# Spatial products moved into the second half of their own batch, thresholds placed by position: threshold attention followed by a gated layer on one core

## The chip, the cores and the metric

One core of a Trainium2 chip (trn2). The metric is the device time of one execution in microseconds. "Span" is the time between first and last instruction of a profiled execution; it is some 2 us shorter than the device time.

In the lines of the profile PE is TensorE (matrix products and transposes), ACT is ScalarE, DVE is VectorE, POOL is GpSimd and SP is the queue that issues DMA. PSUM is the memory into which PE writes its results. The *granted clock* is the share of TensorE's full clock that the profile shows as granted.

## The reference, cut to what matters

Shapes: 8 batches, 8 heads, 576 positions, head size 64; the gated layer maps 512 to 1024 and back to 512.

```python
scores = scale * q @ k^T                                  # per head, 576 x 576
thresh = max(scores, -1) - tau                            # keep what lies within tau of the maximum
attn = softmax(where(scores >= thresh, scores, -1e9))
x = (attn @ v)                                            # heads side by side: 576 x 512 per batch
h = relu(x @ w_in); u, v = h[:, :512], h[:, 512:]
v_n = (v - mean(v)) / sqrt(var(v) + 1e-6)
v_s = w_spatial @ v_n + b_spatial                         # 576 x 576 over positions
out = (u * v_s) @ w_out
```

## The kernel before: the parts that matter

Attention runs in 144 steps: 32 pairs of heads, each with blocks c = 0 to 3 of 128 query rows, and one step c = 4 for the remaining 64 rows of every two pairs. Four pairs make a batch, hence 18 steps per batch. I call the place of a step within its batch its *position*, 0 to 17: pair 0 has 0 to 3, pair 1 has 4 (c = 4) and 5 to 8, pair 2 has 9 to 12, pair 3 has 13 (c = 4) and 14 to 17.

Into these steps the gated layer of an earlier batch is woven as small jobs on PE: v (five jobs: values and their normalization), u (five), s (five spatial products) and o (four output products). Each job takes a bank of PSUM from a pool of **two**, and the bank is free again when an engine has copied the result out:

```python
ps_f = ctx.enter_context(tc.tile_pool(name="ps_f", bufs=2, space=PSUM))   # two banks for all jobs
ps_s = inner.enter_context(tc.tile_pool(name="ps_s", bufs=2, space=PSUM)) # two score tiles of three banks

ORDER = "vsvsvsvssuvuouououo"      # one job per step from step LAG = 26 on, 19 in 18 steps
for b in range(B):
    for j, t in enumerate(ORDER):
        g = LAG + PER * b + j      # step; position (j + 8) % 18
        job = (f, b - (t in "so"), n[t])    # s and o belong to the batch before
```

A step issues its scores, then its jobs; copies by ScalarE ("act") and VectorE ("dve") stand at fixed places:

```python
def step(i, c, fs):
    s = scores(i, c)
    for kind, mm, ev in fs[:2]:            # the first two jobs, one bank each
        mm()
        if kind == "act": ev()             # ScalarE copies, behind what it has queued already
    nc.vector.tensor_reduce(out=nm, in_=s, op=ALU.max, negate=True)
    # ... VectorE copies of the first two jobs; delayed squares of v ...
    if on_act(i, c):                       # threshold on ScalarE: Prelu twice, one Exp of 1152
        # ...
    else:                                  # Exp twice; VectorE masks in the next step
        # ...
    if unmasked: mask()                    # VectorE, for the step before
    for kind, mm, ev in fs[2:]:            # a third job needs the first job's bank
        mm()
        # ...

def on_act(i, c):
    return c in (2, 4) or c == 0 and 0 < i < 6
```

After step 143 the *tail* runs what is left of batches 6 and 7, with eight banks, as many as the two job banks and the two score tiles of three banks make in the steps.

## Time and profile before

Median 481.5 us of 4 runs (480.25 to 484.56). I cut the run at the starts of the row maximum on VectorE, of which each step has exactly one:

| stretch | us | what it holds |
|---|---|---|
| start to step 26 | 78.2 | attention of batch 0 and half of 1 |
| steps 26 to 43 | 52.6 | first batch of the gated layer, without s and o before the change |
| steps 44 to 133, per 18 steps | 55.4 | five full batches |
| step 134 to the last maximum | 28.5 | a half period |
| last maximum to the end | 41.3 | the tail |

A period holds 47 to 50 us of ScalarE's and VectorE's work and 52.8 of PE's. The lines are in the prediction.

### The profile page before, as it was taken

How to read it: one execution, taken by the hardware profiler on the slowest of the kernel's cores; microseconds unless marked ns; L12 is line 12 of the kernel's file. 1: busy time of each engine (PE TensorE's matmuls, PEld its weight loads, DVE VectorE, ACT ScalarE, POOL GpSimd, SP SyncE). 2: the span in 40 equal slices, each digit the busy share in tenths (PEclk: the TensorE clock that was granted, in tenths of full speed). 3: DMA queues.
4: the chain of work that ended last, by engine and by line, in shares of the span. 5: the costliest groups of instructions: out<-in, count | busy, mean ns of one | idle time of the engine just before them, and what ended most of it. 6: DMA issues, size and time to landing. Idle time of an engine off the chain costs nothing.

```text
span 477.7 us, 9895 instructions
## 1 busy us (share of the span) xinstructions
PE 447.0 (94%) x3646; PEld 239.6 (50%) x3691; DVE 410.2 (86%) x563; ACT 389.9 (82%) x677; POOL 225.9 (47%) x403
## 2 busy tenths in 40 slices
PE   7788888889999999999999999999999999999995
PEld 5344444445545555454555545545554545545542
DVE  4989888989889988999889989899889998898573
ACT  4899899989879897888979798788978888897251
POOL 3553344895448543574417642565336744252021
PEclk9999999999999999999999999999999999999999
DMA  7989999979888899988978998998997989777522
GB/s 242 238 182 184 217 221 219 196 148 210 172 182 194 196 210 219 196 172 173 215 192 199 181 206 191 204 171 180 200 225 171 186 183 212 149 113 111 150 95 104
DMA packets 227568, 88.49 MB, mean 185 GB/s; under 512 B 197056, under 2 KB 221760, under 8 KB 227520
## 3 DMA queue, kind: packets, MB, share of 16 engines
q1 hardware_dynamic: 226864, 86.98, 85.4%
q8 instruction: 29, 0.48, 0.4%
q0 software_dynamic: 160, 0.52, 0.3%
q10 hardware_dynamic: 496, 0.36, 0.2%
q14 instruction: 19, 0.16, 0.1%
HBM read 33.31 MB, written 9.44 MB: 89 GB/s over the span
## 4 chain that ended last, share of the span: by engine, by line
PE 49%; ACT 22%; DVE 20%; issue 6%; DMA 2%; POOL 0%; POOLq 0%; DVEq 0%; ACTq 0%
PE s L566 14%; DVE negm L604 10%; DVE p L585 7%; ACT e L621 6%; ACT e L627 5%; PE f L294 4%; PE f L245 4%; PE s L561 4%; PE f L535 4%; PE f L476 3%; ACT sq L458 2%; ACT vrel L444 2%; ACT p L623 2%; PE f L506 2%; PE f L289 2%
## 5 line engine op out<-in xcount | busy, mean ns | idle before, releaser
L604 DVE TENSOR_REDUCE negm<-s 128x2 f32<-128x1152 f32 x144 | 194.8, 1353 | 32.2 <-PE s L566 31.8
L566 PE MATMUL s<-qkT 64*128 64x512 f32 (+1 forms) x640 | 161.9, 636 | 0.0
L585 DVE SCALAR_TENSOR_TENSOR p<-e,ctau 128x1152 bf16<-128x1152 f32 x91 | 133.5, 1468 | 1.2 <-ACT e L627 1.2
L627 ACT ACTIVATE e<-s,negm 128x576 f32<-128x576 f32 x182 | 124.9, 741 | 6.2 <-DVE negm L604 6.0
L621 ACT ACTIVATE e<-s,negm 128x576 f32<-128x576 f32 x106 | 73.0, 743 | 14.4 <-DVE negm L608 9.3
L561 PE MATMUL s<-kd,qkT 128*128 128x128 f32 (+1 forms) x320 | 64.5, 304 | 12.1 <-ACT e L627 6.6
L268 POOL COPY kd<-qkT 64x64 f32<-64x64 f32 x62 | 28.2, 455 | 99.5 <-ACT qkT L263 97.7
L561 PEld LDWEIGHTS s<-kd,qkT 128*128 128x128 f32 (+1 forms) x320 | 44.2, 179 | 30.9 <-ACT e L627 15.7
L566 PEld LDWEIGHTS s<-qkT 64*128 64x128 f32 (+1 forms) x640 | 41.9, 174 | 18.2 <-issue 2.7
L452 POOL TENSOR_SCALAR nmean<-sm 128x1 f32<-128x1 f32 (+1 forms) x35 | 15.7, 449 | 68.4 <-ACT vrel L444 61.5
L294 PEld LDWEIGHTS <-pT 128*128 128x128 bf16 x1024 | 41.8, 97 | 8.0 <-issue 5.6
L294 PE MATMUL f<-v,pT 128*128 128x65 bf16 x992 | 44.9, 194 | 0.0
L623 ACT ACTIVATE p<-e 128x1152 bf16<-128x1152 f32 x37 | 43.0, 1163 | 1.2
L136 POOL COPY qn<-ql 128x640 f32<-128x640 f32 x31 | 33.5, 1081 | 16.4 <-DMA ql<-in_k_dram 11.5
L464 POOL TENSOR_SCALAR vn<-vrel,rs,nm 128x512 bf16<-128x512 f32 (+1 forms) x34 | 29.9, 880 | 3.7
L289 PE MATMUL f<-v,pT 128*128 128x130 bf16 x124 | 27.2, 219 | 4.4 <-ACT qkT L252 2.3
L506 PE MATMUL f<-wsT,vn 128*128 128x512 bf16 x119 | 30.7, 379 | 0.3
L252 ACT COPY qkT<-f 128x512 f32<-128x512 f32 x31 | 18.3, 589 | 14.8 <-PE f L245 14.8
L476 PE MATMUL f<-xT,w_in 128*128 128x512 bf16 x97 | 27.8, 381 | 1.6 <-DVE xn L303 0.8
L303 DVE TENSOR_TENSOR xn<-f,r 128x256 bf16<-128x256 f32 x62 | 26.3, 425 | 2.1
L434 PE MATMUL f<-w_in,xT 128*128 128x512 bf16 x102 | 27.5, 380 | 0.3
L444 ACT ACTIVATE vrel<-f 128x512 f32<-128x512 f32 (+1 forms) x34 | 20.1, 592 | 7.4 <-PE f L260 3.0
(168 smaller groups left out, 642.9 us busy)
## 6 DMA issues: line engine op xcount, KB each, us to landing
vl<-in_v_dram SPq DMA_DIRECT2D x16, 512.0 KB, 4.5
ql<-in_q_dram SPq DMA_DIRECT2D x15, 512.0 KB, 4.5
kl<-in_k_dram SPq DMA_DIRECT2D x15, 512.0 KB, 4.5
out_dram<-o SPq DMA_DIRECT2D x20, 256.0 KB, 3.2
uT<-in_moe_w_in_dram SPq DMA_DIRECT2D x3, 512.0 KB, 6.2
uT<-in_moe_w_spatial_dram SPq DMA_DIRECT2D x2, 576.0 KB, 5.1
vl<-in_v_dram SPq DMA_DIRECT2D x16, 64.0 KB, 4.3
pT<-p SPq DMA_TRANSPOSE x64, 5.5
```

What stands on the lines that cost most here:

```text
L136: nc.gpsimd.tensor_copy(out=t, in_=ld_ring[i // 2 % 2][w][:, 2 * (i % 2):2 * (i % 2) + 2].rearrange("p h c d -> p c h d"))
L289: nc.tensor.matmul(out=t[:, at:at + 130], lhsT=pt[:, 4, :], rhs=vt[:, 4:6, :].rearrange("p b d -> p (b d)"), start=True, stop=False)
L294: nc.tensor.matmul(out=t[:, at + 65 * h:at + 65 * h + 65], lhsT=pt[:, 5 * h + j, :], rhs=vt[:, 6 * h + j, :], start=False, stop=(h == 1 an ...
L476: nc.tensor.matmul(out=t, lhsT=w_in[:, m, f * P:(f + 1) * P], rhs=xts[b][:, m, 0:512], start=(m == 0), stop=(m == 3))
L506: nc.tensor.matmul(out=t, lhsT=vn[:, c, f * P:(f + 1) * P], rhs=wsT[:, c, 0:512], start=(c == 0), stop=(c == 4))
L561: nc.tensor.matmul(out=view(s[rows], 512, [[448, 2], [1, 64]]), lhsT=qks[n][:, 0, m], rhs=kd_ring[n % 2], start=True, stop=True)
L566: nc.tensor.matmul(out=s[rows, 1024 * h:1024 * h + 512], lhsT=qks[n][hs, 0, m], rhs=qks[n][hs, 1, 0:512], start=True, stop=True)
L585: nc.vector.scalar_tensor_tensor(out=pt[:, c % 2, :], in0=ef, scalar=ctau, in1=ef, op0=ALU.is_ge, op1=ALU.mult)
L604: nc.vector.tensor_reduce(out=nm, in_=s, axis=AX.X, op=ALU.max, negate=True)
L621: nc.scalar.activation(out=e[:, h, :], in_=s[:, h, :], func=ACT.Prelu, bias=nm[:, h:h + 1], scale=by, alpha=1e30)
L623: nc.scalar.activation(out=pr_ring[i // 2 % 2] if c == 4 else p_ring[2 * (i % 2) + c // 2][:, c % 2], in_=e.rearrange("p h s -> p (h s)"), ...
L627: nc.scalar.activation(out=e[:, h, :], in_=s[:, h, :], func=ACT.Exp, bias=nm[:, h:h + 1])
```

## The change

The intent: let the spatial products of a batch follow in the second half of its own 18 steps, beside the u jobs, and put its output products beside the next batch's v jobs, so that the tail has less left; and put ScalarE's thresholds (which relieve VectorE) into the half where the spatial products load VectorE. The spatial weights must then be ready earlier.

```diff
-        return c in (2, 4) or c == 0 and 0 < i < 6
+        return c == 4 or (c in (0, 2) and i % 4 < 2 if i > 6 else c == 2 or c == 0 and 0 < i < 6)
 ...
-                   ((20, 25, 30), load_ws), ((24, 26, 29, 31, 34), shape_ws),
-                   ((36, 41, 46, 51), load_w_o), ((39, 44, 49, 54), shape_w_o)):
+                   ((19, 22, 28), load_ws), ((23, 25, 27, 30, 33), shape_ws),
+                   ((32, 34, 37, 40), load_w_o), ((35, 38, 41, 44), shape_w_o)):
 ...
-    ORDER = "vsvsvsvssuvuouououo"
+    ORDER = "vovovovovuuusususss"
 ...
-            if t in "uv" or b:
+            if t != "o" or b:
-                job = (f, b - (t in "so"), n[t])
+                job = (f, b - (t == "o"), n[t])
 ...
-        jobs.setdefault((29, 33, 34, 42, 44)[j], []).append((ws_pe, j))
+        jobs.setdefault((29, 31, 33, 35, 36)[j], []).append((ws_pe, j))
 ...   (and the tail's list: batch 6's s jobs come out of ORDER, o and the last v are gone)
```

Per period the thresholds at positions 11 and 16 go to VectorE and those at 0 and 5 go to ScalarE.

More of the change, by code (lines that the diff above doesn't have):

```diff
@@ L860 @@
         run(last[0], pv_rest(NPAIR // 2 - 1), *last[1:3], x_pe(NPAIR - 2), *last[3:6],
-            pv(NPAIR - 1, 0), *last[6:], pv(NPAIR - 1, 1), moe_s(Z - 1, 0), moe_s(Z - 1, 1),
-            x_pe(NPAIR - 1, True), *[moe_s(Z - 1, j) for j in range(2, 5)])
+            pv(NPAIR - 1, 0), last[6], pv(NPAIR - 1, 1), last[7], x_pe(NPAIR - 1, True), last[8])
+        assert len(last) == 9
         rest = last_gmlp(Z)
```

## The prediction

> **What bounds the kernel now.** I read the page first: the engines' shares, then the chain that ended last.
>
> ```profile
> PE 447.0 (94%) x3646; PEld 239.6 (50%) x3691; DVE 410.2 (86%) x563; ACT 389.9 (82%) x677; POOL 225.9 (47%) x403
> ...
> PE 49%; ACT 22%; DVE 20%; issue 6%; DMA 2%; POOL 0%; POOLq 0%; DVEq 0%; ACTq 0%
> ```
>
> Three engines are nearly full and the chain passes among them. The next question is whether 94% on PE is real. The list of the chain in order of time shows the loop: the same piece of PE work comes back once per batch.
>
> ```profile
> 245.98 1.09 PE f L506 x5
> ...
> 301.19 1.08 PE f L506 x5
> ...
> 356.83 1.09 PE f L506 x5
> ...
> 412.04 1.09 PE f L506 x5
> ```
>
> The distances are 55.2, 55.6 and 55.2 us: one batch of attention, 18 steps, with one batch of the gated layer woven in. The table by stretches cuts the run there (cuts are at starts of the row maximum on DVE, one per step):
>
> ```profile
> 78.23:130.85 52.62, 48.18 (x418) 26.77 (x423) 47.30 (x59) 47.77 (x88) 33.76 (x57) 1.00 0.89 185
> ...
> 241.85:297.06 55.21, 54.16 (x442) 28.83 (x448) 49.38 (x64) 47.43 (x85) 27.59 (x49) 1.00 0.91 194
> ...
> 437.80:477.70 39.90, 34.38 (x275) 17.61 (x276) 22.06 (x53) 15.36 (x29) 5.57 (x7) 1.00 0.42 119
> ```
>
> The columns are length, then busy time of PE, weight load, DVE, ACT, POOL. The first row is the only batch period without spatial and output products (there is no batch before the first); the last row is the tail after the last step, where the rest of the gated layer runs alone.
>
> Because PE's ends are modelled, I priced PE by distances between starts in its timeline, two in the loop and six in the tail:
>
> ```profile
> 271.31 0.46 PE L561 MATMUL s<-kd,qkT 128*128 128x128 f32 x2
> ...
> 272.76 0.66 PE L245 MATMUL f<-identf,qn 128*128 128x128 f32 x4
> ```
> ```profile
> 440.34 1.03 PE L476 MATMUL t<-xT,w_in 128*128 128x512 bf16 x4
> 441.21 1.03 PE L535 MATMUL t<-w_o,gT 128*128 128x512 bf16 x4
> 442.07 1.03 PE L476 MATMUL t<-xT,w_in 128*128 128x512 bf16 x4
> ...
> 449.88 1.24 PE L506 MATMUL f<-wsT,vn 128*128 128x512 bf16 x5
> 450.96 0.75 PE L511 MATMUL f<-wsT,vn 128*128 128x64 bf16 x20
> 451.76 3.40 PE L661 MATMUL t<-w_in,xT 128*128 128x512 bf16 x15
> ```
>
> The scores of a step take 1.45, a u, v or o job 0.86, an s job 1.08 (its last, of 64 columns, 0.59; the last u 0.47), a weighing with the values 0.60, the transposes for one pair 1.04. Per period: 18 x 1.45 + 10 x 0.60 + 4 x 1.04 + v 4.3 + u 3.9 + s 4.9 + o 3.4 = 52.8. So **PE is occupied for about 52.8 of 55.2 to 55.6 us**, and idles only 2.3 to 2.8 per period. In the tail it hardly idles until its last product.
>
> **What the Trainium skill says.** "Perfetto Trace Analysis", section "Identifying the Most-Contended Engine", warns that matmul busy time is no measure of headroom; hence the pricing by starts. Here it agrees with the busy column within 1.4 us per period. "TensorE: Matmul & The Clock Gate", section "Back-to-back issue gap", gives N/2.4 + 2.5 ns for an isolated matmul (216 ns at 512 columns), and 131 ns sustained. The trace has 0.86/4 = 215 ns in a stream, so the first figure holds here and the second doesn't: no hidden speed is left in PE. "ScalarE: Activation LUTs", section "What ACT_TABLE_LOAD costs", gives 186 + 0.833 N ns with immediate operands: 1146 ns for the thresholding Exp of 1152 elements, against 1163 in the trace. "Perfetto Trace Analysis", section "Matmuls", asks that groups rotate through banks so that evacuation overlaps; only two such banks serve these jobs here, and most of PE's small waits are for one (0.44 and 0.37 us per period before the third job of two steps).
>
> **The change, part by part.**
>
> ```profile
> L604 DVE TENSOR_REDUCE negm<-s 128x2 f32<-128x1152 f32 x144 | 194.8, 1353 | 32.2 <-PE s L566 31.8
> ...
> L585 DVE SCALAR_TENSOR_TENSOR p<-e,ctau 128x1152 bf16<-128x1152 f32 x91 | 133.5, 1468 | 1.2 <-ACT e L627 1.2
> ...
> L623 ACT ACTIVATE p<-e 128x1152 bf16<-128x1152 f32 x37 | 43.0, 1163 | 1.2
> ```
>
> *Thresholds by position.* A step thresholded on ACT costs ACT 1.16 more and DVE about 1.42 - 0.2 less. Counting the condition over the 32 pairs: before, 32 (c=2) + 5 (c=0) + 16 (c=4) = 53 steps; after, for i up to 6, 7 + 5, for later pairs 12 x 2, and 16: 52. The totals don't move (7 of 18 steps per period in both); only the place does: they now lie in the half of the batch that holds u and s.
>
> *Order.* The 19 jobs of a period stay the same: PE's 52.8 us remain. What moves is DVE's load: before, two neighbouring steps (the eighth and ninth of the order) hold maximum, mask, weighing and spatial gating, 1.35 + 1.42 + 0.75 + 0.69 = 4.2 and 1.35 + 1.42 + 0.2 + 0.6 + 0.42 = 4.0 us of DVE, 8.2 against 6.4 of PE. In the trace they take 4.1 and 3.7 us between row maxima, against a mean of 3.08. Afterwards the heaviest such pair is 2.8 + 4.3 = 7.1 of DVE against 6.9 of PE. A sum of the largest load over every two neighbouring steps falls by 0.6 us per period; over three or more steps it is even. I take **-0.5 per period**, over 5.5 periods: **-2.8**.
>
> *First batch.* Its five spatial products (4.9 us of PE) move from after it into its own period. That one had 48.5 of work in 52.6; it gets 53.4 and should take 55.5 or so: **+3.0**. The weights' loads, a few steps earlier, are small beside that.
>
> *Tail.* Of batch 6, the tail keeps u1 to u4 and its five s jobs, and loses the last v job and four o jobs: 5 x 0.86 = 4.3 of PE; the half period before it gets 0.6 lighter (it holds v and o, not v and s). That is the same 4.9 us that went to the first batch. Not all comes back, though. The view of the mean's readers shows this:
>
> ```profile
> L452 POOL TENSOR_SCALAR nmean<-sm x35: 182/192/1415, 79.3 to 439.8; 128x1 f32<-128x1 f32 x28, 64x1 f32<-64x1 f32 x7
> L458 ACT ACTIVATE sq<-vrel,nmean x34: 708/711/734, 84.5 to 431.1; 128x512 bf16<-128x512 f32 x28, 64x512 bf16<-64x512 f32 x6
> ```
>
> Seven last-rows means, but six squares: the delayed normalization of batch 6's last v job is queued after the queue was emptied, so the kernel before never executes it and uses stale rows (too small an effect on the output to notice, by the 0.01/576 weights). Now that job is in the last but one step, and its normalization does run, behind the last step's Exp (done at about 439.2): square 0.9, then POOL's small operations 1.0 and the 0.8 us write, so about 442.3. The first s job can come as early as 436.3 + 0.86 + 0.60 + 0.86 = 438.6 and its fifth product must wait: **2.8 us of PE idle**, in place of the work that left. The last transposed weights land at 445.7 in the trace, which then binds no more. Net for the end: -4.3 - 0.6 + 2.8 + 0.5 for the shorter cover of the last transposes = **-1.6**.
>
> Sum: 482.5 - 2.8 + 3.0 - 1.6 = 481.1. I shade this to 480.5, as my tail wait could be partly covered.
>
> **Rivals.** (a) *The balance pays fully*: if DVE's heavy steps cause most of PE's 2.3 to 2.8 us of idling per period, 5.5 periods give up to -14, or 468. Against it: those waits are spread over a dozen places of 0.05 to 0.44 us, mostly bank evictions by ACT, which the change doesn't remove. (b) *A new collision*: v with its square and o are all ACT's, so in the first half ACT's evictions come later; or the step with v, weighing and s wants a third bank. Another 0.5 us per period would give 486. For it: two banks only; against: before has as many three-job steps. (c) *The tail gives all 4.9 us and the first batch hides its own*: 475 or so; against: the first batch's period has just 4.0 us of PE idle, and the normalization wait. (d) *DMA*: its share is 0.89 to 0.95 in loop stretches; transposes already are late now and then (0.6 us in one period), but no bytes are added.
>
> **Range and chances.** Balance -8 to +4, first batch +2 to +4, end -4.5 to 0, the runs themselves 480 to 485: 474 to 486. Faster by over 2% needs 472.9, nearly all of PE's idling removed: 0.08. Slower needs 492: 0.04.
>
> **What would show it.** Period: spacing of the repeated s job between 54.3 and 55.4. First batch: its 18 steps near 55.5. Tail from the last Exp: about 38 us, with PE waiting some 2 to 3 us in the first s job for POOL's vn, and 7 squares of 64 rows. The prediction is wrong if the period changes by over 1 us either way, or if PE's work per period isn't a floor.

## More of the kernel before

The copy that frees the first bank at positions 6 and 15 is that of `qk_rem`, a small transpose of q and k's remaining rows (L263 in the profile). The third job there is `pv_rest` (L289 and L294), the weighing (the product of attention weights and values) for the remaining rows.

## The result

The changed kernel took **503.36 us** (median of 4, 501.14 to 505.5) against 481.5: ratio 1.0444, 95% interval 1.037 to 1.0518, slower. (A ratio is the mean time of one kernel's fast runs over that of the other's of the same rounds, so not quite the ratio of the medians.) The output is correct.

The page of the changed kernel, engines' shares and chain:

```profile
PE 456.0 (91%) x3691; PEld 240.8 (48%) x3691; DVE 415.3 (83%) x561; ACT 391.0 (78%) x680; POOL 226.3 (45%) x407
...
PE 56%; ACT 21%; DVE 17%; issue 5%; POOL 1%; POOLq 0%; ACTq 0%
```

The engines do nearly the same work in a longer span, so all shares fall. The table by stretches, with the same cuts as before (length, then busy PE, weight load, DVE, ACT, POOL, then granted clock and DMA):

```profile
79.31:139.75 60.44, 52.99 (x449) 28.98 (x448) 48.42 (x63) 51.00 (x90) 32.42 (x59) 1.00 0.82 171
...
198.04:256.34 58.30, 54.92 (x450) 28.88 (x449) 50.66 (x65) 47.37 (x85) 27.87 (x49) 1.00 0.87 185
...
460.35:500.40 40.05, 32.77 (x266) 16.65 (x264) 21.93 (x52) 13.96 (x27) 7.77 (x11) 0.96 0.35 93
```

Of 22.7 us of span, five periods took 14.4 (58.3 each, not 55.4), the first batch 7.8 (60.4, not 52.6), the start 1.1, the half period -0.7, the tail 0.1. The start is not counted for or against the change: kernels whose code is the same up to step 33 measured 78.2 (before) and 82.5 (position 16 to 5, below) there. In nine of the fifteen profiled runs, the changed kernel's among them and not the kernel before's, PE's clock is granted at 0.50 for 3.4 or 6.8 us somewhere between 18 and 32 us. In the periods the sum of PE's distances between starts that hold no wait is 53.0 (52.8 before), so the added time is **waiting of PE**: 5.3 us per period, 2.3 to 2.8 before. Two waits make most of it: 1.70 us at position 6 and 1.26 at position 15, before the third job. Here is position 6 in the kernel before, PE then ACT:

```profile
290.16 0.33 PE L260 MATMUL f<-identf,qn 128*128 128x128 f32 x1
290.33 1.03 PE L535 MATMUL f<-w_o,gT 128*128 128x512 bf16 x4
291.19 0.22 PE L289 MATMUL f<-v,ptr 128*128 128x130 bf16 x1
```
```profile
289.53 1.38 ACT L627 ACTIVATE e<-s,negm 128x576 f32<-128x576 f32 x2
290.78 0.28 ACT L263 COPY qkT<-f 128x128 f32<-128x128 f32 x1
```

The small transpose (L260) takes bank A, the output product bank B, and the weighing (L289) needs A again. ScalarE copies A out behind its Exp pair, in time: the weighing starts 0.86 us after the job before, with no wait. The same position in the changed kernel, PE then ACT:

```profile
305.56 0.33 PE L260 MATMUL f<-identf,qn 128*128 128x128 f32 x1
305.72 1.24 PE L506 MATMUL f<-wsT,vn 128*128 128x512 bf16 x5
308.50 0.22 PE L289 MATMUL f<-v,ptr 128*128 128x130 bf16 x1 [1.53 <-ACT qkT L263]
```
```profile
305.73 1.37 ACT L621 ACTIVATE e<-s,negm 128x576 f32<-128x576 f32 x2 [0.55 <-DVE negm L608]
307.13 1.16 ACT L623 ACTIVATE p<-e 128x1152 bf16<-128x1152 f32 x1
308.20 0.25 ACT L263 COPY qkT<-f 128x128 f32<-128x128 f32 x1
```

The step before, position 5, now has its threshold on ScalarE, so an Exp of 1.16 us (L623) lies between the pair and the copy. The job in bank B has issued its last product (5 x 0.215 us after 305.72), and PE waits until 308.50 with the bracket naming the copy. Counted from the transpose (L260), the copy starts after 2.64 us, where it was 0.62 before. Of these 2.02 us the Exp is 1.16; most of the rest, 0.8, is that the pair itself starts later, as it had to wait for VectorE's row maximum (the bracket of 0.55).

### The profile page after: what moved, and what is told of

Read it like the earlier page. It is cut to its first block, busy times and chain, and to the rows that moved or that the text cites. A ratio compares the mean times of both kernels' runs of the same rounds, so it can differ in the third digit from the quotient of the medians.

```text
span 500.4 us, 9964 instructions
## 1 busy us (share of the span) xinstructions
PE 456.0 (91%) x3691; PEld 240.8 (48%) x3691; DVE 415.3 (83%) x561; ACT 391.0 (78%) x680; POOL 226.3 (45%) x407
## 4 chain that ended last, share of the span: by engine, by line
PE 56%; ACT 21%; DVE 17%; issue 5%; POOL 1%; POOLq 0%; ACTq 0%
PE s L566 18%; DVE negm L604 8%; PE s L561 6%; ACT e L621 6%; DVE p L585 5%; PE f L245 5%; PE f L294 4%; PE f L434 4%; ACT e L627 4%; PE f L476 3%; PE f L506 3%; ACT p L623 3%; PE f L535 3%; ACT sq L458 2%; ACT vrel L444 2%
## 5 line engine op out<-in xcount | busy, mean ns | idle before, releaser
L566 PE MATMUL s<-qkT 64*128 64x512 f32 (+1 forms) x640 | 163.8, 642 | 0.0
L585 DVE SCALAR_TENSOR_TENSOR p<-e,ctau 128x1152 bf16<-128x1152 f32 x92 | 135.1, 1470 | 5.8 <-ACT e L627 5.6
L268 POOL COPY kd<-qkT 64x64 f32<-64x64 f32 x62 | 15.5, 250 | 123.5 <-ACT qkT L263 121.8
L464 POOL TENSOR_SCALAR vn<-vrel,rs,nm 128x512 bf16<-128x512 f32 (+1 forms) x35 | 43.1, 1232 | 3.8
L623 ACT ACTIVATE p<-e 128x1152 bf16<-128x1152 f32 x36 | 41.9, 1163 | 1.1
L452 POOL TENSOR_SCALAR nmean<-sm 128x1 f32<-128x1 f32 (+1 forms) x35 | 12.9, 368 | 61.1 <-ACT vrel L444 61.1
L250 ACT ACTIVATE qkT<-f 128x512 f32<-128x512 f32 x31 | 18.3, 590 | 16.3 <-PE f L245 16.3
L136 POOL COPY qn<-ql 128x640 f32<-128x640 f32 x31 | 23.9, 772 | 14.1 <-DMA ql<-in_k_dram 10.4
L289 PE MATMUL f<-v,pT 128*128 128x130 bf16 x126 | 27.8, 220 | 2.5 <-ACT xT L374 1.4
L476 PE MATMUL f<-xT,w_in 128*128 128x512 bf16 x104 | 26.8, 380 | 2.5 <-ACT wsT L408 2.5
L434 PE MATMUL f<-w_in,xT 128*128 128x512 bf16 x112 | 28.9, 380 | 0.0
```

The costliest lines, as they stand in the source:

```text
L434: nc.tensor.matmul(out=t, lhsT=xts[b][:, f, c * P:(c + 1) * P], rhs=w_in[:, f, 512:1024], start=(f == 0), stop=(f == 3))
L464: nc.gpsimd.tensor_scalar(out=dst, in0=vrel[:n], scalar1=rs[:n], scalar2=nm[:n], op0=ALU.mult, op1=ALU.add)
L476: nc.tensor.matmul(out=t, lhsT=w_in[:, m, f * P:(f + 1) * P], rhs=xts[b][:, m, 0:512], start=(m == 0), stop=(m == 3))
L566: nc.tensor.matmul(out=s[rows, 1024 * h:1024 * h + 512], lhsT=qks[n][hs, 0, m], rhs=qks[n][hs, 1, 0:512], start=True, stop=True)
L585: nc.vector.scalar_tensor_tensor(out=pt[:, c % 2, :], in0=ef, scalar=ctau, in1=ef, op0=ALU.is_ge, op1=ALU.mult)
L623: nc.scalar.activation(out=pr_ring[i // 2 % 2] if c == 4 else p_ring[2 * (i % 2) + c // 2][:, c % 2], in_=e.rearrange("p h s -> p (h s)"), ...
```

## The experiments

All are correct. First the pieces of the change, one at a time.

**Thresholds alone.**

```diff
--- before
-        return c in (2, 4) or c == 0 and 0 < i < 6
+        return c == 4 or (c in (0, 2) and i % 4 < 2 if i > 6 else c == 2 or c == 0 and 0 < i < 6)
```

> The kernel before with the new thresholds by position alone. Theory T (the moved thresholds put 1.16 us of ScalarE work ahead of the eviction that frees the bank for the third job of a step): the spacing of batches rises from 55.4 us by 1 us or more, total 488 to 496. Rival O (the new order is the cause, by its neighbours): the spacing stays within 0.5 us of 55.4, total 479 to 485.

497.09 us, ratio 1.0318 (1.0255 to 1.038). A period takes 58.1 us. The third jobs wait 1.23 us at position 6 (none before) and 1.04 at position 15 (0.44 before). One line of the waits within a period names it (idle time in total, times, longest, in us; the modelled ends of matmuls make these shorter than the distances between starts that I quote):

```profile
PE f L289 <- ACT qkT L263: 1.9, 2, 1.1
```

So moving two thresholds per period without any new work costs 2.7 us per period: theory T. Besides the two third jobs (1.23 and 0.60 more), a transpose at position 14 waits 0.74 on average for a bank that VectorE frees; theory T doesn't name that one.

**Order alone.** The changed kernel with the old `on_act`.

```diff
--- after
-        return c == 4 or (c in (0, 2) and i % 4 < 2 if i > 6 else c == 2 or c == 0 and 0 < i < 6)
+        return c in (2, 4) or c == 0 and 0 < i < 6
```

> The changed kernel with the old thresholds. Theory T: the 1.70 us wait before the weighing of the remaining rows (third job of the step with a scores transpose and a spatial product) falls below 0.6, the spacing is 55.2 to 56.8 instead of 58.3, total 484 to 492. Rival O: the spacing stays above 57.5, total 497 to 504. In both the first batch's 18 steps stay near 60 us, as order and weights are as in the changed kernel.

488.95 us, ratio 1.0153 (1.0103 to 1.0202). A period takes 56.1 us, the wait at position 6 is 0.30 in three of five periods (0.37 on average), at 15 it is 0.89. The first batch takes 59.6. Both came as theory T had it: the order costs 0.7 per period, but 7.0 in the first batch. Thresholds and order alone give 13.7 + 3.6 us over five periods, 14.4 together, so their waits partly coincide.

**Weights early alone.** The kernel before with the new steps for the weights' loads, casts and transposes (the second to fourth pairs of lines of the diff above, ORDER kept).

```diff
--- before
-                   ((20, 25, 30), load_ws), ((24, 26, 29, 31, 34), shape_ws),
+                   ((19, 22, 28), load_ws), ((23, 25, 27, 30, 33), shape_ws),
 ...
-        jobs.setdefault((29, 33, 34, 42, 44)[j], []).append((ws_pe, j))
+        jobs.setdefault((29, 31, 33, 35, 36)[j], []).append((ws_pe, j))
```

> The kernel before with only the weights' loads, casts and transposes at the earlier steps. If packing them is what makes the first batch's 18 steps cost 7.8 us more where I had priced 3.0, these 18 steps go from 52.6 to 54.5 or more, total +2 us or more; if not (spatial products and thresholds do it), they stay within 0.7 us of 52.6.

481.79 us, ratio 1.0004 (0.9959 to 1.0049): no change in all, where the expectation had +2 us or more if the packing mattered. The first batch does take 55.3 (+2.7), but the next period takes 54.0 (-1.3), as the loads of the output weights and one transpose have left it, and the interval hides the rest. A stage can lose what the total doesn't show.

**Each threshold move alone**, to see what makes it costly. Position 16 to 5 first:

```diff
--- before
-        return c in (2, 4) or c == 0 and 0 < i < 6
+        return c in (2, 4) and not (i > 6 and i % 4 == 3 and c == 2) or c == 0 and (0 < i < 6 or i > 6 and i % 4 == 1)
```

> The kernel before with one of the two threshold moves: for pairs after the sixth, the one of the last pair of a batch (position 16) goes to VectorE and the c=0 of its second pair (position 5, just ahead of a step with three jobs) to ScalarE. Bank theory: the 1.16 us Exp delays the copy that frees the bank of the third job at position 6: a wait of 1.0 to 1.7 us appears there where the kernel before has none, spacing 56.3 to 57.5. Rival (VectorE overload where thresholds were taken away): no wait at position 6, spacing up only if waits appear at positions 15 to 17.

490.23 us (one run; the kernel before had 480.5 beside it), 56.5 per period. At position 6, PE then ACT:

```profile
298.28 1.03 PE L535 MATMUL f<-w_o,gT 128*128 128x512 bf16 x4
300.38 0.22 PE L289 MATMUL f<-v,ptr 128*128 128x130 bf16 x1 [1.07 <-ACT qkT L263]
```
```profile
299.01 1.16 ACT L623 ACTIVATE p<-e 128x1152 bf16<-128x1152 f32 x1
300.08 0.25 ACT L263 COPY qkT<-f 128x128 f32<-128x128 f32 x1
```

A wait of 1.24 us (start distance 2.10 less 0.86) where there was none; all others are as before. ScalarE has no pause here: pair, Exp and copy follow each other. This is the bank theory's sign at the place that it named. (The total of this single run says less: its start, which the edit doesn't touch, took 4.3 us longer than in the profile of the kernel before.) Then position 11 to 0:

```diff
+        return c in (2, 4) and not (i > 6 and i % 4 == 2 and c == 2) or c == 0 and (0 < i < 6 or i > 6 and i % 4 == 0)
```

> The other move: position 11 to VectorE, position 0 to ScalarE. Overload theory: VectorE has 1.4 us more at positions 12 to 13, beside spatial products, its maxima come later, and the third job at position 15 waits about 1.0 us (0.44 before); spacing 56 to 57. Rival (only the place before a three-job step matters): spacing within 0.4 of 55.4.

490.4 us (one run), 57.0 per period. Position 15 waits 1.04 us, and position 14 waits 0.62 on average for a bank that VectorE frees. In one period, ACT at position 13, then PE at position 14:

```profile
265.06 1.37 ACT L621 ACTIVATE e<-s,negm 128x576 f32<-128x576 f32 x2 [2.20 <-DVE r L301]
```
```profile
265.64 0.63 PE L245 MATMUL f<-identf,qn 128*128 128x128 f32 x4 [0.65 <-DVE xn L303]
```

Position 0 isn't followed by a three-job step; the loss is on the other side: VectorE keeps the mask of position 11 and is late into the spatial products and weighings of positions 11 to 15, its maxima hold up ScalarE (2.20 us in the line above), and with it the copy. The two moves add 1.1 and 1.6 us per period; both 2.7.

**The copy that frees the bank, on another engine.** If the thresholds act only through ScalarE's late copy, they should cost nothing once VectorE makes that copy. One kernel has the new thresholds, its control the old ones.

```diff
--- thresholds alone; and, for the control, before
-            nc.scalar.copy(out=qks[i][:, :, 512:576],
+            nc.vector.tensor_copy(out=qks[i][:, :, 512:576],
                           in_=hold["t"][:, 0:P].rearrange("p (w s) -> p w s", w=2))
```

> Thresholds alone, and the copy of the remaining rows' transpose (which frees the first bank of both three-job steps) done by VectorE instead of ScalarE. Bank theory: the waits of 1.23 and 1.04 us before the third job fall below 0.4 each, spacing from 58.05 to 56.8 or less, total 488 to 491. Rival (VectorE's own overload sets the pace): VectorE gets 4 copies of some 0.3 us more, spacing 58 or more, total 496 or more.

> The control: the same copy on VectorE in the kernel before, whose third job waits 0.44 us at one of the two steps. Bank theory: within 0.5 us per period of before either way, total 478 to 484. If eviction by ScalarE costs before as well, it is faster by up to 3 us.

490.53 us (ratio 1.0215, 1.0155 to 1.0275) with the new thresholds, 490.22 (1.0192, 1.0134 to 1.0251) with the old. Here **both placements of the thresholds take 57.1 us per period**. With the new thresholds the kernel gains 6.6 us of the medians against thresholds alone, and no third job waits for L263 any more; the total came as the bank theory asked, the fall of 1.0 us per period fell short of its 1.2. The equality is a balance of different waits, so it doesn't show that the thresholds act through ScalarE's copy alone: with the new ones PE waits 0.88 at position 14 and 0.84 at 16, with the old ones not at all at 14, but 0.99 at 16 and 0.61 at 17. The control went against the theory: VectorE's extra copies cost before 1.7 us per period, as its own copies for other jobs then come late (the 0.99 us stands before a weighing). The two banks are a shared resource, and both copying engines are short of time.

**The shorter job in front.** In the kernel before a wait of 0.37 us stands at position 7, where the short u job of 0.47 us precedes the third job.

```diff
--- before
+            nth = (0, 1, 2, 4, 3)[n[t]] if t == "u" else n[t]
-                job = (f, b - (t in "so"), n[t])
+                job = (f, b - (t in "so"), nth)
```

> The kernel before with the short u job (64 columns, 0.47 us) exchanged with the 0.86 us one before it, so that the long one stands in front of the third job of position 7. Bank theory: the wait of 0.37 us there falls to 0.05 or less and spacing by up to 0.4 us, total 478 to 480. Rival (PE's small waits are slack that another engine takes up at once): spacing within 0.1 us, total unchanged.

479.89 us, ratio 1.0007 (0.9978 to 1.0035). The wait is gone and a period takes 55.1 instead of 55.4: most of a PE wait turns into time (0.28 of 0.37). The tail, whose order also changed, gave 1.2 us back, so the total shows nothing.

**First batch and tail of the new order.** Three kernels on the order with the old thresholds. The first lets VectorE copy the weights' transposes, and in the tail puts the spatial product later:

```diff
--- order alone
-            nc.scalar.copy(out=wsT[:, :, c * P:(c + 1) * P],
+            nc.vector.tensor_copy(out=wsT[:, :, c * P:(c + 1) * P],
 ...
-        run(last[0], pv_rest(NPAIR // 2 - 1), *last[1:3], x_pe(NPAIR - 2), *last[3:6],
-            pv(NPAIR - 1, 0), last[6], pv(NPAIR - 1, 1), last[7], x_pe(NPAIR - 1, True), last[8])
+        run(last[0], pv_rest(NPAIR // 2 - 1), last[1], last[3], x_pe(NPAIR - 2), last[5],
+            pv(NPAIR - 1, 0), last[2], last[4], last[6], pv(NPAIR - 1, 1), last[7],
+            x_pe(NPAIR - 1, True), last[8])
```

> The changed kernel with the old thresholds, and two mends that act in different stages: the spatial weights' transposes are copied out of their bank by VectorE instead of ScalarE (first batch), and in the tail the first spatial product of batch 6 comes after all four u jobs and one weighing (tail). Bank theory for the first batch: the waits of 1.6, 1.2, 1.2 and 1.5 us behind these transposes fall by 3 us or more in sum, its 18 steps from 59.6 to 56.5 or less; rival (they are just too much work): 58.5 or more. Tail: PE no longer waits 2.2 us for POOL's normalization and the granted clock stays at 1.00; from the last row maximum to the end 36 to 38 us instead of 40.1 to 41.4; rival (the last transposed weights take over as the bound): 39 or more. Total 481 to 485, against 489.

487.44 us, ratio 1.0155 (1.0124 to 1.0186). The first batch took 60.3, no better than 59.6: the waits only moved (1.35 and 0.96 us for banks that VectorE frees). So there changing the copying engine doesn't help; it makes other copies late. In the tail the wait for POOL is gone, but one of 1.2 us for the last transposed attention weights took its place; it takes 39.1 from the last maximum, 40.1 in the order alone: the rival, in the main. The granted clock was 1.00 there. The total, 481 to 485 expected, was missed.

The second transposes the weights by DMA, so that these jobs leave PE, ScalarE and the banks (same tail):

```diff
--- order alone
-    for j in range(5):
-        jobs.setdefault((29, 31, 33, 35, 36)[j], []).append((ws_pe, j))
+    ws_at = dict(zip((29, 31, 33, 35, 36), range(5)))
 ...
+            if g in ws_at:
+                sends.append(lambda c=ws_at[g]: nc.sync.dma_start_transpose(
+                    out=wsT[:, :, c * P:(c + 1) * P], in_=wsb[:, c, :]))
```

> New order, old thresholds, the tail with the later first spatial product, and the spatial weights transposed by DMA, so that the first batch has no such jobs on PE and ScalarE (1.4 us of PE, 3.6 us of ScalarE and five third jobs less). Packing theory: the waits of PE at steps 31 to 37 fall by 3 us or more and the first batch's 18 steps go from 59.6 (60.3 with VectorE's copies) to 56.5 or less, total near 484. Rival (the first batch is late for other causes, the spatial products themselves or DMA): 58.5 or more.

485.8 us, ratio 1.0091 (1.0044 to 1.0139). The waits at steps 31 to 37 fall from 5.5 to 2.1 us, but the first spatial product waits 2.4 us: 58.8, which by its number is the rival (58.5 or more, with DMA as one of its causes). The fourth transpose was issued at 110.86, the slowest of the five landed 5.0 us after its issue (2.8 in the median), and the product goes on at 116.00; so I take it that the product waited for this one, though the profile's bracket names ScalarE. This wait shows something else. The table by stretches around it (granted clock after POOL):

```profile
114.00:116.00 2.00, 0.00 (x1) 0.04 (x2) 1.64 (x3) 1.96 (x4) 0.00 (x0) 1.00 1.28 229
116.00:118.00 2.00, 1.78 (x5) 0.94 (x7) 0.00 (x0) 1.02 (x1) 1.63 (x3) 0.54 1.07 238
118.00:120.00 2.00, 2.00 (x7) 0.79 (x5) 0.69 (x1) 0.00 (x0) 1.04 (x3) 0.60 0.79 100
```

After PE's pause its clock is granted at 0.54 and 0.60 in two slices of 2 us; from 116.20 to 119.50 it is 0.50. Over 3.4 us half a clock is some 1.7 us of work, by estimate. Not every pause has this after it; see the last section.

The third issues these transposes sooner, at steps 25, 27, 29, 32 and 34, and moves the last weighing of the tail behind one more spatial product, and the last transpose to the end of the list:

> New order, old thresholds, the spatial weights transposed by DMA as before but issued two to four steps sooner, so that the fourth lands ahead of the first spatial product; in the tail the last weighing comes one spatial product later. If packing of the weights' jobs is what the first batch lost beyond its 4.9 us of products, its 18 steps go from 58.8 to 56.3 or less (no wait of 2.6 us at step 38); if the products and the four us of PE's idling were mis-sized for another cause, 57.5 or more. Tail from the last row maximum 38.3 or less (the wait of 1.2 us for the last transposed weights falls below 0.3). Total 479 to 483.

482.69 us, ratio 1.0044 (1.0012 to 1.0075). The first batch takes 56.8, between the two expectations: 2.8 of the 59.6 was the packing of the weights' jobs, and a wait of 1.67 us for transposed attention weights that come by DMA remains. The tail takes 38.0, as expected.

**The output copies on VectorE**, on top of the second of these:

```diff
--- order, weights by DMA
-            (nc.scalar.copy if not wide or c % 2 == 0 else nc.vector.tensor_copy)(
+            (nc.scalar.copy if wide and c % 2 == 0 else nc.vector.tensor_copy)(
 ...
-        return "act", mm, ev
+        return "dve", mm, ev
```

> The same, and the output products copied out of their bank by VectorE, which lost the spatial products' evictions in this half, instead of ScalarE, which got the output products. Theory for the order's part (ScalarE runs late in the half with v, square and o, so the third job at position 15 waits 0.89 us for its bank, 0.44 before): that wait falls to 0.5 or less and the spacing from 56.1 to 55.5 or less, total 480 to 482. Rival (only the shorter middle job, 0.86 against 1.08 us, counts): the wait stays at 0.6 or more and the spacing at 55.9 or more.

485.89 us, ratio 1.0097 (1.0064 to 1.013). The wait at position 15 is 0.65 in four of five periods and 1.26 in one (0.89 without), that at position 6 stays at 0.32 on average, and a period takes 56.5: the rival. Who copies the output isn't why the order costs 0.7 per period. With the new order the job between first and third at position 15 is 0.86 us and not 1.08, which leaves 0.22 more of the wait uncovered; the rest of the 0.7 stays unassigned.

**What the experiments point to**, tried on the kernel before: weights' transposes by DMA (at steps 27, 29, 32, 34, 37), and the short u job early in all batches but the last two, so that the tail stays.

```diff
--- before
+            nth = (0, 1, 2, 4, 3)[n[t]] if t == "u" and b < B - 2 else n[t]
 ...   (weights by DMA as above)
```

> The kernel before with the spatial weights transposed by DMA and the short u job ahead of the long one in all batches but the last two. If the weights' jobs on PE and ScalarE cost the first batch a bank each, its 18 steps fall from 52.6 by 1 to 2 us; spacing as with the exchange alone, 55.0 to 55.4; total 477 to 479, the fastest of all. Rival: the transposes on the DMA queue delay those of the scores, and nothing is won: 480 or more.

**478.03 us**, ratio 0.9963 (0.9927 to 0.9998), the fastest of all, by 0.4%, with an interval that barely leaves out no change. Its first batch takes 51.9 (0.7 less, not 1 to 2), its periods 54.9.

All kernels side by side, stretches of the profiled run in us:

| kernel | start to step 26 | first batch | mean of five periods | half | tail | span |
|---|---|---|---|---|---|---|
| before | 78.2 | 52.6 | 55.4 | 28.5 | 41.3 | 477.7 |
| after | 79.3 | 60.4 | 58.3 | 27.8 | 41.4 | 500.4 |
| thresholds alone | 78.7 | 56.1 | 58.1 | 29.4 | 41.6 | 496.5 |
| order alone | 80.9 | 59.6 | 56.1 | 27.1 | 40.1 | 488.4 |
| weights early | 79.6 | 55.3 | 55.2 | 28.5 | 41.3 | 480.4 |
| position 16 to 5 | 82.5 | 53.5 | 56.5 | 28.3 | 41.5 | 488.4 |
| position 11 to 0 | 79.7 | 53.1 | 57.0 | 29.6 | 41.3 | 488.6 |
| thresholds, copy on VectorE | 78.6 | 53.8 | 57.1 | 29.5 | 41.4 | 488.8 |
| before, copy on VectorE | 78.0 | 54.4 | 57.1 | 29.1 | 41.3 | 488.4 |
| before, short u early | 78.4 | 52.3 | 55.1 | 28.6 | 42.5 | 477.5 |
| order, weights' copy on VectorE | 78.6 | 60.3 | 56.2 | 26.9 | 39.1 | 485.7 |
| order, weights by DMA | 78.6 | 58.8 | 56.2 | 26.8 | 38.9 | 484.0 |
| the same, output on VectorE | 78.8 | 57.8 | 56.5 | 27.3 | 39.8 | 486.1 |
| order, weights by DMA sooner | 79.9 | 56.8 | 56.3 | 27.0 | 38.0 | 483.1 |
| before, weights by DMA, short u | 79.1 | 51.9 | 54.9 | 28.6 | 40.8 | 474.9 |

## Why the prediction was wrong, step by step

**Per period: -0.5 predicted, +2.9 measured. This is the step that failed**, and it made 14.4 of the 22.7 us. PE's work per period was right (53.0 against 52.8). What failed was how I took the idle time: I summed each engine's load over neighbouring steps, saw it even, and gave VectorE's fall from 8.2 to 7.1 us in its worst pair a gain of 0.5. So the wait was mispriced, and with the wrong sign: -0.5 was forecast, and the waits grew by 2.5 to 3.0. Such a sum doesn't see *where in a queue* a copy stands. The prediction had the right lines in hand: that most of PE's small waits are for one of two banks, and (rival b) that ScalarE's copies could come later or a step could want a third bank. It set them at 0.5 us per period, "before has as many three-job steps". The number of such steps stayed; what changed is what ScalarE has to do just ahead of the copy. The threshold of position 5 with its 1.16 us Exp, moved by itself, made a wait of 1.24 us at position 6; the relief taken from position 11 made 0.6 more at 15 and as much at 14, and there no Exp was added ahead of the copy: VectorE was late. (Both figures are from the kernel before with one move; with the new order position 14 has no wait.) With that copy on VectorE the waits for it were gone, and both placements took the same time, with other waits. "Perfetto Trace Analysis", section "Optimization Strategy", says that a gap that recurs on the engine that should be saturated can mean too few PSUM buffers for the next tile. The trace agrees as to the gap: 1.70 and 1.26 us, at the same two positions in every period. That a third bank would have removed it is not shown; no run had one, as job banks and score tiles take all eight that the kernel has.

In a smaller point the text was also wrong: ScalarE has six thresholds per period in both kernels, not seven. The count of 53 and 52 in all was right.

**First batch: +3.0 predicted, +7.8 measured.** That its five spatial products come in was right. I let 4.0 us of PE's idling absorb part of them and called the earlier weights small. The weights' jobs, four of which make a third job in their step, cost 2.7 by themselves (weights early), and taking them off PE gave 2.8 back; the thresholds added 0.8 (60.4 against 59.6). The longest wait there is the same step failing once more. At step 37 a job needs the bank of the last transposed weights, and ScalarE has the thresholding Exp of step 36 (a position 0) ahead of the copy:

```profile
116.19 1.02 PE L476 MATMUL f<-xT,w_in 128*128 128x512 bf16 x4 [2.54 <-ACT wsT L408]
```
```profile
114.39 1.16 ACT L623 ACTIVATE p<-e 128x1152 bf16<-128x1152 f32 x1
115.46 0.67 ACT L408 COPY wsT<-f 128x640 bf16<-128x640 bf16 x1
```

By starts this wait is 2.70 us, and 1.50 in the order alone, where that Exp is not. With the weights' jobs off PE and the old thresholds, about 1.3 us over the predicted 55.5 remains, not settled, with a DMA wait of 1.67 in that trace.

**Tail: -1.6 predicted, counting the half period's -0.6, and -0.6 measured.** The mechanism is as described; the size of the sum is in part luck, as follows. The changed kernel has 35 squares, 7 of them of 64 rows: the normalization that the kernel before drops now runs. Its first spatial product issues four of five products and waits for it (PE of the changed kernel, then of the order alone):

```profile
462.31 1.03 PE L506 MATMUL t<-wsT,vn 128*128 128x512 bf16 x4
465.41 0.39 PE L506 MATMUL t<-wsT,vn 128*128 128x512 bf16 x1 [2.07 <-POOL vn L464]
```
```profile
452.02 0.81 PE L506 MATMUL t<-wsT,vn 128*128 128x512 bf16 x3
455.07 0.39 PE L506 MATMUL t<-wsT,vn 128*128 128x512 bf16 x1 [2.23 <-POOL vn L464]
```

I predicted 2 to 3 us, 2.8 in the sum. That sum has a slip: 439.2 + 0.9 + 1.0 + 0.8 is 441.9, not 442.3, which leaves 2.4. And two errors offset each other: POOL's operations and write took 2.8 us (462.5 to 465.4), not 1.8, while the spatial product came later against the last Exp (0.5 us after its end, not 0.6 before). In the first of the two the pause was followed by a lower clock, which I had not considered:

```profile
466.00:468.00 2.00, 2.00 (x8) 0.71 (x6) 0.53 (x1) 1.18 (x2) 0.00 (x0) 0.57 0.98 182
468.00:470.00 2.00, 2.00 (x22) 1.18 (x21) 0.41 (x1) 0.00 (x0) 0.00 (x0) 0.58 0.00 0
```

From the last Exp's end to the end of the run it took 38.6 us; the order alone, with the same wait and no drop in clock, took 36.6; the kernel before 38.5. So the tail's own step, -1.0 without the half period, lies between what was measured with the drop (+0.1) and without (-1.9; -1.2 counted from the last maximum). Of the 2.0 us between the two, the clock of 0.50 over 3.4 us explains about 1.7, by estimate.

**Rivals.** (a) and (c) didn't occur. (b) did, about six times as large as I made it. (d), DMA, played a part only at single places.

## What to carry to other kernels

When all engines are near full and jobs rotate through two banks, moving work to a less loaded engine isn't free because the sums are even: look at each copy that frees a bank, at what stands ahead of it in that engine's queue, and at what the next user of the bank has to cover the delay with. Test such a move one place at a time, because a single 1.16 us instruction put ahead of the wrong copy shows up as a wait of about its own length in every period. And where PE pauses on an otherwise full stretch, look at the clock granted after it: in four of nine pauses here it fell to 0.50 for 3.4 us.

## What the Trainium skill lacked or had wrong

- "Perfetto Trace Analysis", section "Matmuls", asks for rotation through banks, but doesn't say that with two banks (as here) a third job waits for the queue of the engine that copies the first out: 1.70 and 1.26 us per period here, 1.24 from one moved instruction.
- "TensorE: Matmul & The Clock Gate", section "What's actually happening", ties the lower clock to an idle window of about 3.4 us. The fifteen profiled runs have nine pauses of PE of over 1.7 us. Four were followed within 1 us of their end by a clock of 0.50 for 3.4 us: 1.73 (thresholds alone, at 126 us), 2.06 (position 16 to 5, at 26), 2.07 (tail of the changed kernel) and 2.44 (first batch with weights by DMA). Five were not: 1.72, 1.84, 2.23 (tail of the order alone), 2.54 (first batch of the changed kernel) and 3.13 (first batch with the output on VectorE). So the length of a pause alone didn't decide it here; what did is not shown.
- The 131 ns per matmul of 512 columns in the same page's section "Back-to-back issue gap" was not reached: 215 ns in the streams of v, u, s and o products at full clock here.
